# Layer norm, hedgehog linear attention and a SwiGLU layer in one kernel: casts of wo, output copies, norms and x stores put at other places in the queues

## The chip, the cores and the metric

The kernel runs on 1 core of one Trainium2 chip. The metric is the device time of one execution, in microseconds (us). The engines of a core are TensorE (PE, with its weight loads PEld), VectorE (DVE), ScalarE (ACT), GpSimd (POOL) and SyncE (SP), which here only issues DMAs. Each engine works through its own queue in order; semaphores make it wait for others.

## The reference

With S = 2048 rows, D = 576, 32 heads of 18 columns, and F = 4608, all in f32:

```python
xn = layernorm(x)                      # no gain, no bias
q, k, v = heads(xn @ wqkv)
pq, pk = q @ w_phi, k @ w_phi          # per head, 18x18
phi_q = concat(softmax(pq), softmax(-pq))
phi_k = concat(softmax(pk), softmax(-pk))
num = phi_q @ (phi_k.T @ v)
den = phi_q @ sum(phi_k) + 1e-6
s = (num / den) @ wo
g = silu((silu(x @ w_gate) * (x @ w_up)) @ w_down)   # this x is the normalised one
out = x + s * g
```

## The kernel before

Every f32 product is made of three products in the format fp32r. A number is split into a high part, which ScalarE casts, and a remainder, which VectorE or GpSimd subtracts (helpers `split`, `split_rows`): most steps below are such a cast and such a subtraction, ahead of matmuls.

The program has these stages, in order of time.

1. **Start, 0 to about 80 us.** x comes in four blocks of four row tiles, in the order 2, 3, 0, 1. For each block, `norm_stats` makes mean and variance on VectorE (bn_stats, L164, and bn_aggr, L165), a square root on ScalarE (L168) and two refinement steps. `norm_block` then normalises two tiles on VectorE (L181) and two on ScalarE (L178), copies the last 64 columns four times over on GpSimd (L184), transposes all on TensorE (L193), casts (ScalarE, L195) and subtracts (VectorE, L196) into the x operands `X`. A `fold` multiplies wk with w_phi (TensorE, L221), and `early_tile` computes tiles of the gate and up products, from weights that `early_weights` loads and splits. Block 2 is called the first block below, and block 3 the second.
2. **Keys and values, to about 228 us.** `k_tile` and `v_product` for 16 row tiles. `keep_x` stores three of the x operands (`a_dram`, 3 x 1280 KB) from SyncE's queue, for the last stage.
3. **Queries, about 228 to 480 us.** `q_tile` makes the feature map of 128 rows; its part `softmax_parts` takes a maximum (L278), a subtraction (L279), the same for the minimum, and two exponentials on ScalarE (L282). `numer` transposes and multiplies, `project` multiplies by wo and copies the output to `s_dram` through a ScalarE copy `so` (L619). `split_wo` casts wo in three pieces (WOH, WOL). Early tiles are laid between.
4. **Gate, up and down, about 480 us to the end.** `gate_up_weights` loads one unit's weights `ld` from SyncE's queue (L676), forms sums on GpSimd (L694 to L697), splits them (`w`) and stores them to `w_dram` (L687) for the second half of the rows; `gate_up` multiplies, with a ScalarE copy `snap` (L736) between products; the down products follow (`strassen`).

The order of each engine's queue is not the order of the text alone: a scheduler chooses among what is ready, and `tc.high_priority()` puts instructions ahead, while `tc.issue_after(x)` holds a group back until instruction x has been placed. Tiles of one name rotate among `bufs` buffers, so a new tile waits for the readers of an old one.

Of the kernel before, what the change touches and what calls it, by code (L numbers as in the profile page):

```python
# [46 lines left out]
def gated_hedgehog_kernel(ctx: ExitStack, tc, x, w_qk, w_v, w_phi, wo, w_gu, w_tail, w_down, ident_in, mask_in, out):  # L47
# [65 lines left out]
    def early_tile(f, i, parts, js=(0, 1), banks=None):  # L113
# [10 lines left out]
        return last  # L124

    with ExitStack() as att:
        const = att.enter_context(tc.tile_pool(name="const", bufs=1))
# [8 lines left out]
        with ExitStack() as wst:  # L136
# [4 lines left out]
            with ExitStack() as pst:  # L141
# [18 lines left out]
                def norm_stats(bs, xns):  # L160
# [11 lines left out]
                    nc.vector.scalar_tensor_tensor(r, q, 1.5, r, op0=ALU.add, op1=ALU.mult)  # L172
                    return nc.vector.scalar_tensor_tensor(q, mv[:, t, 0], -1.0, r, op0=ALU.mult, op1=ALU.mult)

                def norm_block(b, xns):
                    for n, (i, xn) in enumerate(zip(range(4 * b, 4 * b + 4), xns)):
                        if n % 2:
                            nc.scalar.activation(xn[:, 0:D], xn[:, 0:D], AF.Identity, bias=rt[:, i:i + 1],  # L178
                                                 scale=rs[:, i:i + 1])
                        else:  # L180
                            nc.vector.tensor_scalar(xn[:, 0:D], xn[:, 0:D], mv[:, i, 0:1], rs[:, i:i + 1],  # L181
                                                    op0=ALU.subtract, op1=ALU.mult)
                        for k in range(2):
                            nc.gpsimd.tensor_copy(xn[:, D + k * P:D + (k + 1) * P].rearrange("p (j n) -> p j n", j=4),  # L184
                                                  xn[:, 512 + 32 * k:544 + 32 * k].unsqueeze(1).to_broadcast([P, 4, 32]))
                    i, j = divmod(b, 2)
                    dst = XB[i][2 * j:2 * j + 2]
                    for c in range(3):
# [5 lines left out]
                        if c < 2:  # L194
                            nc.scalar.copy(dst[c][:, 0:2], ps)  # L195
                            nc.vector.tensor_sub(dst[c][:, 3:5], ps, dst[c][:, 0:2])  # L196
                            continue
# [75 lines left out]
            def softmax_parts(ps, e):  # L273
# [7 lines left out]
                for s in range(2):  # L281
                    nc.scalar.activation(e[:, s * D:(s + 1) * D], e[:, s * D:(s + 1) * D], AF.Exp,  # L282
                                         scale=1.0 if s == 0 else -1.0)
# [4 lines left out]
            kk_pool, read = kk, []  # L288

# [9 lines left out]
            def keep_x():  # L299
                for n, j in enumerate((0, 1, 3)):  # L300
                    nc.sync.dma_start(a_dram[n], XB[1][j].bitcast(F32))
# [17 lines left out]
            def sum_parts(k):  # L319
                r = raws[k]  # L320
                lo = los[k] = kk.tile([P, 4, 2, P], F32R, name="slo", bufs=1)
                for a in (2, 0):
# [5 lines left out]
                    nc.sync.dma_start(sum_dram[k // 4, :, j, k % 4, 0:3], hi.bitcast(F32))  # L328
                    nc.sync.dma_start(sum_dram[k // 4, :, j, k % 4, 3:5], lo[:, j].bitcast(F32))

# [97 lines left out]
            for p in range(8):  # L428
# [93 lines left out]
        with ExitStack() as qst:  # L522
# [75 lines left out]
            def project(b, oh, ol, last):  # L598
                for j in range(QS // P):
# [3 lines left out]
                    for i in range(2):  # L603
# [8 lines left out]
                        for g, (o, w) in enumerate(GROUPS):  # L612
                            for a, bw in ((oh, WOH), (oh, WOL), (ol, WOH)):
                                nc.tensor.matmul(ps[:, 0:HALF], a[0:w, g, jc], bw[0:w, g, n], start=k == 0,  # L614
                                                 stop=k == 3 * NG - 1)
                                k += 1
                        so = qk.tile([P, HALF], F32, name="so", bufs=2)
                        with tc.high_priority() if last else ExitStack():
                            nc.scalar.copy(so, ps[:, 0:HALF])  # L619
                        nc.scalar.dma_start(s_dram[r0:r0 + P, n], so)  # L620
# [408 lines left out]
    early_tile(EARLY - 1, 0, parts)  # L1029
    ready = [gate_up_weights(*todo.pop(0))]  # L1030
    est.close()
# [74 lines left out]
```

## Time and profile before

| | |
|---|---|
| time, median of 3 runs | 1636.75 us (1635.69 to 1640.77) |
| the profiled execution | 1638.38 us, its span 1636.6 us |
| TensorE busy | 1604.0 us (98%) |
| VectorE busy | 1168.5 us (71%) |
| ScalarE busy | 721.9 us (44%) |
| GpSimd busy | 653.3 us (40%) |
| DMA | 268.46 MB, mean 164 GB/s |

The span is the time from the first to the last instruction on the engines; 1.8 us of the execution lie around it. Busy times are sums over the whole span, and the stages differ: TensorE is without idle time for most of the program, and its idle time lies in a few places.

### The profile page before, as it was taken

To read this page: it belongs to the slowest core of one execution; us is meant where nothing else is said; L and a number is where in the kernel's file an instruction comes from. 1 tells how busy PE (TensorE), PEld (TensorE's weight loads), DVE (VectorE), ACT (ScalarE), POOL (GpSimd) and SP (SyncE) were. 2 spreads that over 40 slices of the span, in tenths; PEclk is the share of its full clock that TensorE was granted. 3 is DMA by queue.
4 is the path that set the end of the run, shared out by engine and by line. 5 is a ranking of instruction groups with operands and counts; after the bars stand their busy time and mean duration, and the time that the engine had idled before them with its cause. 6 is when DMAs were issued, how large, how long until landed. Compare 5 with 4: busy or idle time off the path is not lost.

```text
span 1636.6 us, 25198 instructions
## 1 busy us (share of the span) xinstructions
PE 1604.0 (98%) x9385; PEld 1429.7 (87%) x9385; DVE 1168.5 (71%) x1721; ACT 721.9 (44%) x1391; POOL 653.3 (40%) x699
## 2 busy tenths in 40 slices
PE   6999998999999999999999999999999999999998
PEld 5899997999978888888888888888888888888887
DVE  7677768899952678778777778825666766666578
ACT  5533345444432554544444544455433433333334
POOL 3485661333212455455545355313233324133132
PEclk9999999999999999999999999999999999999999
DMA  9622243334248545555554554684454655555444
GB/s 286 206 80 78 85 134 117 117 103 126 67 144 306 184 165 175 179 178 168 177 180 165 175 192 152 224 296 150 136 162 135 199 184 170 172 179 185 140 115 174
DMA packets 121741, 268.46 MB, mean 164 GB/s; under 512 B 12787, under 2 KB 53363, under 8 KB 119827
## 3 DMA queue, kind: packets, MB, share of 16 engines
q1 hardware_dynamic: 106652, 246.49, 45.9%
q0 software_dynamic: 3072, 11.02, 2.4%
q10 hardware_dynamic: 11894, 9.35, 1.8%
q8 instruction: 74, 1.21, 0.3%
q14 instruction: 49, 0.39, 0.1%
HBM read 167.19 MB, written 99.61 MB: 163 GB/s over the span
## 4 chain that ended last, share of the span: by engine, by line
PE 90%; DMA 4%; DVE 3%; POOL 1%; issue 1%; ACT 1%; SPq 0%; ACTq 0%; POOLq 0%; DVEq 0%
PE px L707 24%; PE pd L832 24%; PE pw L707 12%; PE py L707 6%; PE p L92 6%; PE pe L92 5%; PE p L614 4%; PE po L594 2%; PE kvp L294 2%; PE vx L382 1%; PE pt L588 1%; DMA xn<-in_A_x 1%; PE vw L382 1%; DMA s_dram<-so 1%; DMA sraw<-in_A_w_v 1%
## 5 line engine op out<-in xcount | busy, mean ns | idle before, releaser
L832 PEld LDWEIGHTS pd<-dw,hh 128*128 128x128 f32 x3048 | 432.4, 188 | 26.4 <-DVE dw L59 1.7
L832 PE MATMUL pd<-dw,hh 128*128 128x288 f32 x3048 | 448.5, 297 | 4.3 <-DVE dw L59 1.5
L707 PE MATMUL px<-X,w 128*128 128x512 f32 x1488 | 384.3, 393 | 0.0
L707 PEld LDWEIGHTS px<-X,w 128*128 128x128 f32 x1488 | 270.6, 188 | 51.8 <-ACT s L736 2.0
L707 PE MATMUL pw<-X,w 128*128 128x512 f32 x732 | 188.7, 393 | 0.0
L707 PEld LDWEIGHTS pw<-X,w 128*128 128x128 f32 x732 | 137.0, 188 | 30.5
L741 DVE TENSOR_TENSOR s<-pw,s 128x512 f32<-128x512 f32 x124 | 85.1, 688 | 100.0 <-ACT s L736 89.2
L957 DVE TENSOR_TENSOR acc<-pd,acc 128x576 f32<-128x576 f32 x128 | 96.2, 752 | 83.8 <-PE pd L832 83.6
L736 ACT COPY s<-px 128x512 f32<-128x512 f32 x124 | 72.6, 585 | 157.2 <-PE px L707 157.2
L92 PE MATMUL pe<-X,wh 128*128 128x512 f32 (+1 forms) x380 | 121.8, 401 | 5.8 <-ACT h L119 2.9
L59 DVE TENSOR_TENSOR hh<-ha,hh 128x512 fp32r<-128x512 f32 x140 | 111.5, 823 | 20.7 <-ACT hh L58 19.1
L58 ACT CAST hh<-ha 128x512 fp32r<-128x512 f32 x140 | 82.7, 619 | 92.4 <-PE pd L832 73.5
L929 POOL TENSOR_TENSOR hb<-hb 128x512 f32<-128x512 f32 x34 | 47.0, 1381 | 168.6 <-DVE hb L753 161.4
L59 DVE TENSOR_TENSOR w<-ld,w 128x512 fp32r<-128x512 f32 (+1 forms) x93 | 77.2, 832 | 35.7 <-ACT w L58 34.5
L707 PE MATMUL px<-X,wt 96*128 96x512 f32 x248 | 97.9, 395 | 0.0
L707 PE MATMUL py<-X,w 128*128 128x512 f32 x372 | 96.5, 394 | 0.0
L916 POOL TENSOR_TENSOR h<-ha,hb 128x512 f32<-128x512 f32 x34 | 44.3, 1302 | 126.8 <-DVE ha L757 88.6
L942 POOL TENSOR_TENSOR ha<-ha 128x512 f32<-128x512 f32 x34 | 52.6, 1564 | 103.5 <-DVE hh L59 103.5
L58 ACT CAST w<-ld 128x512 fp32r<-128x512 f32 (+1 forms) x93 | 51.0, 549 | 89.6 <-POOL ld L697 56.8
L92 PEld LDWEIGHTS pe<-X,wh 128*128 128x128 f32 (+1 forms) x380 | 70.0, 189 | 21.7 <-ACT h L119 3.4
L761 ACT COPY py<-px 128x512 f32<-128x512 f32 x62 | 35.5, 572 | 102.7 <-PE px L707 80.8
L707 PEld LDWEIGHTS py<-X,w 128*128 128x128 f32 x372 | 66.7, 188 | 11.2
(262 smaller groups left out, 3199.0 us busy)
## 6 DMA issues: line engine op xcount, KB each, us to landing
w_dram<-w SPq DMA_DIRECT2D x90, 512.0 KB, 2.9
w<-w_dram SPq DMA_DIRECT2D x90, 512.0 KB, 4.5
wt<-t_dram SPq DMA_DIRECT2D x61, 336.0 KB, 3.7
ld<-in_B_w_gu SPq DMA_DIRECT2D x31, 512.0 KB, 4.5
X<-sum_dram SPq DMA_DIRECT2D x8, 1280.0 KB, 11.1
rt<-in_B_w_down SPq DMA_DIRECT2D x33, 288.0 KB, 3.1
rb<-in_B_w_down SPq DMA_DIRECT2D x33, 288.0 KB, 4.7
w_dram<-w SPq DMA_DIRECT2D x30, 256.0 KB, 2.1
```

Source lines behind the costliest of these rows:

```text
L58: nc.scalar.copy(hi, src)
L59: nc.vector.tensor_sub(lo, src, hi)
L92: last = nc.tensor.matmul(ps, l, r, start=n == 0, stop=n == len(pairs) - 1)
L614: nc.tensor.matmul(ps[:, 0:HALF], a[0:w, g, jc], bw[0:w, g, n], start=k == 0, stop=k == 3 * NG - 1)
L707: nc.tensor.matmul(ps, l, r, start=first and n == 0, stop=last and n == len(mm) - 1, skip_group_check=True)
L736: nc.scalar.copy(t, ps)
L741: nc.vector.tensor_add(t, ps, t)
L832: nc.tensor.matmul(ps, l, r, start=first and n == 0 and m == 0, stop=n == len(hs) - 1 and m == 2, skip_group_check=True)
L916: sub(s, g["h"][0][0], g["h"][0][1])
L929: nc.gpsimd.tensor_add(a21, a21, g["h"][1][1])
L942: sub(a12, a12, g["h"][0][0])
L957: nc.vector.tensor_add(a2, pd[:, :, 0:HALF], a2)
```

## The change

Five things are edited.

- `norm_block` runs its norms (L178, L181, L184) with priority.
- The second block's `norm_stats` is held back until the first block's last remainder (L196) is placed, in place of the last step of the first block's statistics; then it runs with priority, and stands ahead of the first early tile's weights in the text.
- `split_wo` is held back until the last exponential placed so far, in place of the last subtraction; the third piece of wo is loaded into a buffer of the name `e` instead of `ez`.
- `keep_x` is held back until the preceding `sum_parts` has been placed.
- The last projection's last two output copies use a buffer of the name `e`, and the first unit's `gate_up_weights` is held back until the last output copy.

```diff
+    outs = []
...
-                    return nc.vector.scalar_tensor_tensor(q, mv[:, t, 0], -1.0, r, op0=ALU.mult, op1=ALU.mult)
+                    nc.vector.scalar_tensor_tensor(q, mv[:, t, 0], -1.0, r, op0=ALU.mult, op1=ALU.mult)
 
                 def norm_block(b, xns):
-                    for n, (i, xn) in enumerate(zip(range(4 * b, 4 * b + 4), xns)):
...
+                    with tc.high_priority():
+                        for n, (i, xn) in enumerate(zip(range(4 * b, 4 * b + 4), xns)):
...
-                            nc.vector.tensor_sub(dst[c][:, 3:5], ps, dst[c][:, 0:2])
+                            rest = nc.vector.tensor_sub(dst[c][:, 3:5], ps, dst[c][:, 0:2])
...
+                    return rest
...
-                chain = norm_stats([2], xns[0:4])
-                norm_block(2, xns[0:4])
+                norm_stats([2], xns[0:4])
+                rest = norm_block(2, xns[0:4])
+                with tc.issue_after(rest.ins), tc.high_priority():
+                    norm_stats([3], xns[4:8])
                 first_weights = [early_weights(0)]
-                with tc.issue_after(chain.ins):
-                    norm_stats([3], xns[4:8])
...
-                    nc.scalar.activation(e[:, s * D:(s + 1) * D], e[:, s * D:(s + 1) * D], AF.Exp,
-                                         scale=1.0 if s == 0 else -1.0)
+                    last = nc.scalar.activation(e[:, s * D:(s + 1) * D], e[:, s * D:(s + 1) * D], AF.Exp,
+                                                scale=1.0 if s == 0 else -1.0)
+                exps.append(last)
...
-                sum_parts(order[p - 1])
+                done = sum_parts(order[p - 1])
                 load_stack(order[p])
                 if p == 3:
-                    keep_x()
+                    with tc.issue_after(done.ins):
+                        keep_x()
...
-                   qk.tile([P, 2, D], F32, name="ez", bufs=1)]
+                   qk.tile([P, 2 * D], F32, name="e", bufs=4).rearrange("p (a n) -> p a n", a=2)]
...
-                with tc.issue_after(read[-1].ins):
+                with tc.issue_after(exps[-1].ins):
                     for n, wr in enumerate(wrs):
...
-                        so = qk.tile([P, HALF], F32, name="so", bufs=2)
+                        if last and i:
+                            so = qk.tile([P, 2 * D], F32, name="e", bufs=4)[:, 0:HALF]
+                        else:
+                            so = qk.tile([P, HALF], F32, name="so", bufs=2)
                         with tc.high_priority() if last else ExitStack():
-                            nc.scalar.copy(so, ps[:, 0:HALF])
+                            outs.append(nc.scalar.copy(so, ps[:, 0:HALF]))
...
-    ready = [gate_up_weights(*todo.pop(0))]
+    with tc.issue_after(outs[-1].ins):
+        ready = [gate_up_weights(*todo.pop(0))]
```

What it does to the queues is read from the order of each engine's instructions. In the rows of the changed kernel the line numbers are its own: from line 126 on they are 1 to 10 higher than those of before.

First the start. VectorE's row, before, at the end of the first block's statistics (`rt` is the bias of the norms on ScalarE, `X_64` and `X_65` are x operands):

```order
L172 SCALAR_TENSOR_TENSOR rs<-rt,rs 128x4
L173 SCALAR_TENSOR_TENSOR rt<-mv,rs 128x4
L181 TENSOR_SCALAR xn<-xn,mv,rs 128x576 x2
L164 BN_STATS stats<-xn 128x6 x2
L196 TENSOR_TENSOR X_64<-tp,X_64 128x1024
L196 TENSOR_TENSOR X_65<-tp,X_65 128x1024
L165 BN_AGGR mv<-stats 128x2
```

and now:

```order
L173 SCALAR_TENSOR_TENSOR rs<-rt,rs 128x4
L183 TENSOR_SCALAR xn<-xn,mv,rs 128x576 x2
L174 SCALAR_TENSOR_TENSOR rt<-mv,rs 128x4
L198 TENSOR_TENSOR X_64<-tp,X_64 128x1024
L198 TENSOR_TENSOR X_65<-tp,X_65 128x1024
L165 BN_STATS stats<-xn 128x6 x3
L166 BN_AGGR mv<-stats 128x2
```

The two norms L181 (now L183) stand ahead of the last step of the statistics L173 (now L174), and the two remainders L196 (now L198) ahead of the second block's first bn_stats.

ScalarE's row there, before, for the second block (its root is L168, its norms are those of `xn_135` and `xn_139`; `wh_346` is the weight of the second early tile, `wst` a piece of w_v):

```order
L168 ACTIVATE rs_104<-mv_103 128x4
L249 CAST KVWH_94<-wst_359 128x576
L249 CAST KVWH_94<-wst_361 128x576
L62 CAST wh_346<-raw_345 128x768
L62 CAST KVWH_94<-tp_274 128x6x126
L62 CAST KVWH_94<-tp_284 128x6x72
L119 ACT_TABLE_LOAD
L119 ACTIVATE h_608<-pe_592 128x512
L178 ACTIVATE xn_135<-xn_135,rt_105,rs_104 128x576
L178 ACTIVATE xn_139<-xn_139,rt_105,rs_104 128x576
```

and now, where the cast of `wh_346` is the row just ahead of these, and the two norms L180 end the piece and follow it:

```order
L119 ACT_TABLE_LOAD
L119 ACTIVATE h_608<-pe_592 128x512
L169 ACT_TABLE_LOAD
L169 ACTIVATE rs_104<-mv_103 128x4
L62 CAST KVWH_94<-tp_274 128x6x126
L62 CAST KVWH_94<-tp_284 128x6x72
L252 CAST KVWH_94<-wst_361 128x576
L252 CAST KVWH_94<-wst_363 128x576
L252 CAST KVWH_94<-wst_365 128x576
L252 CAST KVWH_94<-wst_367 128x576
L252 CAST KVWH_94<-wst_369 128x576
L180 ACTIVATE xn_135<-xn_135,rt_105,rs_104 128x576
```

The root, now L169, has moved behind the cast of `wh_346`, a SiLU and two table loads, and five casts of w_v stand ahead of the norms.

Second the first query tiles. VectorE's row before (`e_2461` is the first tile's result, `h_4768` the product of an early tile):

```order
L278 TENSOR_REDUCE m_2462<-p2_2432 128x32
L279 TENSOR_TENSOR e_2461<-p2_2432,m_2462 128x576
L278 TENSOR_REDUCE m_2462<-p2_2432 128x32
L279 TENSOR_TENSOR e_2461<-p2_2432,m_2462 128x576
L122 TENSOR_TENSOR h_4768<-pe_4753,h_4768 128x512
L63 TENSOR_TENSOR wl_4788<-raw_4786,wh_4787 128x512
```

and now:

```order
L281 TENSOR_REDUCE m_2462<-p2_2432 128x32
L122 TENSOR_TENSOR h_4768<-pe_4753,h_4768 128x512
L282 TENSOR_TENSOR e_2461<-p2_2432,m_2462 128x576
L281 TENSOR_REDUCE m_2462<-p2_2432 128x32
L282 TENSOR_TENSOR e_2461<-p2_2432,m_2462 128x576
L63 TENSOR_TENSOR wl_4788<-raw_4786,wh_4787 128x512
```

The product L122 has moved between the first maximum, L278 (now L281), and its subtraction, L279 (now L282).

Third the first units of the last stage. SyncE's row before (`ld_5468` holds the third unit's weights):

```order
L123 DMA h_dram_69<-h_5285 128x512
L676 DMA ld_5468<-in_B_w_gu 128x4x256
L123 DMA h_dram_69<-h_5319 128x512
L890 DMA rt_5560<-in_B_w_down 128x576
L890 DMA rb_5562<-in_B_w_down 128x576
L890 DMA rt_6118<-in_B_w_down 128x576
L890 DMA rb_6120<-in_B_w_down 128x576
L687 DMA w_dram_72<-w2_5383 128x1024
L687 DMA w_dram_72<-w2_5387 128x1024
L676 DMA ld_5566<-in_B_w_gu 128x4x256
```

and now:

```order
L696 DMA w_dram_72<-w2_5350 128x1024
L696 DMA w_dram_72<-w2_5354 128x1024
L696 DMA w_dram_72<-w1_5358 128x512
L696 DMA w_dram_72<-w2_5374 128x1024
L696 DMA w_dram_72<-w2_5383 128x1024
L696 DMA w_dram_72<-w2_5387 128x1024
L696 DMA w_dram_72<-w1_5391 128x512
L685 DMA ld_5468<-in_B_w_gu 128x4x256
L732 DMA ha_5463<-h_dram_69 128x512
L732 DMA hb_5464<-h_dram_69 128x512
```

The load of `ld_5468`, L676 (now L685), has moved behind all stores of the first two units' weights to `w_dram`.

More of the change, by code (lines that the diff above doesn't have):

```diff
@@ L172, in norm_stats @@
                     nc.vector.scalar_tensor_tensor(r, q, 1.5, r, op0=ALU.add, op1=ALU.mult)
-                    return nc.vector.scalar_tensor_tensor(q, mv[:, t, 0], -1.0, r, op0=ALU.mult, op1=ALU.mult)
+                    nc.vector.scalar_tensor_tensor(q, mv[:, t, 0], -1.0, r, op0=ALU.mult, op1=ALU.mult)
                 def norm_block(b, xns):
-                    for n, (i, xn) in enumerate(zip(range(4 * b, 4 * b + 4), xns)):
[L177 to L185, printed above, removed]
+                    with tc.high_priority():
+                        for n, (i, xn) in enumerate(zip(range(4 * b, 4 * b + 4), xns)):
+                            if n % 2:
+                                nc.scalar.activation(xn[:, 0:D], xn[:, 0:D], AF.Identity, bias=rt[:, i:i + 1],
+                                                     scale=rs[:, i:i + 1])
+                            else:
+                                nc.vector.tensor_scalar(xn[:, 0:D], xn[:, 0:D], mv[:, i, 0:1], rs[:, i:i + 1],
+                                                        op0=ALU.subtract, op1=ALU.mult)
+                            for k in range(2):
+                                nc.gpsimd.tensor_copy(xn[:, D + k * P:D + (k + 1) * P].rearrange("p (j n) -> p j n", j=4),
+                                                      xn[:, 512 + 32 * k:544 + 32 * k].unsqueeze(1).to_broadcast([P, 4, 32]))
                     i, j = divmod(b, 2)
@@ L286, in softmax_parts @@
                 return sm
-            kk_pool, read = kk, []
+            kk_pool, read, exps = kk, [], []
             def kv_step(n, phi, v):
@@ L328, in sum_parts @@
                     nc.sync.dma_start(sum_dram[k // 4, :, j, k % 4, 0:3], hi.bitcast(F32))
-                    nc.sync.dma_start(sum_dram[k // 4, :, j, k % 4, 3:5], lo[:, j].bitcast(F32))
+                    done = nc.sync.dma_start(sum_dram[k // 4, :, j, k % 4, 3:5], lo[:, j].bitcast(F32))
+                return done
             V1, V2 = slice(D + HALF, 2 * D), slice(D, D + HALF)
```

1 line of the change is left out of this document (added).

## The prediction

> **What bounds the kernel now.** The page comes first: the busy line of the engines.
>
> ```profile
> PE 1604.0 (98%) x9385; PEld 1429.7 (87%) x9385; DVE 1168.5 (71%) x1721; ACT 721.9 (44%) x1391; POOL 653.3 (40%) x699
> ```
>
> TensorE is busy for 1604.0 of 1636.6 us, so all that any reordering can win is the other 32.6 us. The second view, the waits of TensorE, says who ends them (columns: total us, times, longest).
>
> ```profile
> PE tp L193 <- DVE xn L181: 11.4, 2, 10.4
> PE pe L92 <- ACT h L119: 2.9, 4, 1.2
> PE pe L92 <- DVE h L122: 1.8, 2, 1.6
> PE tp L221 <- DVE X L196: 1.8, 1, 1.8
> PE pd L832 <- DVE dw L59: 1.5, 1, 1.5
> PE p L92 <- DVE e L279: 1.4, 1, 1.4
> PE p L614 <- ACT so L619: 1.2, 1, 1.2
> PE pd L832 <- DVE hh L59: 1.1, 1, 1.1
> ```
>
> 10.4 us of the first row is the wait for the first x rows, which the edit does not shorten. What it can reach is the rest of these rows, about 11.7 us. The third view, the windows, says where the rest of the program stands (span start:end, length, PE busy, then PEld, DVE, ACT, POOL, granted clock, DMA share, GB/s).
>
> ```profile
> 260.00:280.00 20.00, 18.08 (x106) 15.59 (x107) 19.62 (x33) 9.84 (x14) 0.00 (x0) 1.00 0.21 67
> 560.00:1636.00 1076.00, 1068.85 (x5876) 942.35 (x5874) 758.10 (x1081) 475.36 (x931) 415.13 (x369) 1.00 0.54 174
> ```
>
> From 560 us on TensorE idles 7.15 us in 1076, nearly all of it at the very end, and the orders of all engines are the same there before and after. So whatever TensorE has gained or lost by 560 us comes out at the end one for one. In 260 to 280 us VectorE is busy for 19.62 of 20: there it is VectorE's order that decides.
>
> The edit reorders three stretches, costed in turn: the start (0 to 80 us), the first query tiles (228 to 275) and the last projection with the first gate-up units (464 to 560).
>
> **The start: what goes.** The timelines of VectorE and of TensorE (start, length, instruction, in brackets the idle time before it and what ended it):
>
> ```profile
> 15.64 0.82 DVE L164 BATCH_NORM_STATS2 stats<-xn 128x6 f32<-128x288 f32 x2 [4.76 <-DMA xn<-in_A_x]
> 16.38 2.34 DVE L196 TENSOR_TENSOR X<-tp,X 128x1024 fp32r<-128x1024 f32 x2
> ...
> 17.64 5.91 PE L221 MATMUL tp<-PHI,wst 126*128 126x126 f32 x36 [1.83 <-DVE X L196]
> 33.47 3.46 PE L193 MATMUL tp<-ident,xn 128*128 128x128 f32 x24 [0.92 <-DVE xn L181]
> 53.58 0.50 PE L92 MATMUL pe<-X,wh 128*128 128x512 f32 x1 [0.82 <-ACT h L119]
> ```
>
> Two bn_stats of the second block, waiting for their DMA until 15.64, stand on VectorE ahead of the two remainders L196, and TensorE's fold waits 1.83 us for the first remainder. In the new order both remainders stand ahead of all bn_stats of that block. Their input is a ScalarE cast:
>
> ```profile
> 9.93 1.63 ACT L178 ACTIVATE xn<-xn,rt,rs 128x576 f32<-128x576 f32 x2 [1.16 <-DVE rt L173]
> 13.07 1.01 ACT L195 CAST X<-tp 128x1024 fp32r<-128x1024 f32 x1 [1.51 <-PE tp L193]
> ```
>
> The norm on ScalarE waits for rt (L173), which now stands behind the two L181, so the chain to this cast is about 1.1 us later: the cast ends at 15.15 instead of 14.08, the first remainder at 15.15 + 1.17 = 16.3, and the fold starts there instead of at 17.64: 1.3 us won. The granted clock adds to it (windows of 2 us, TensorE alone):
>
> ```profile
> 16.00:18.00 2.00, 0.36 (x3) 1.00 1.01 384
> 18.00:20.00 2.00, 2.00 (x16) 0.72 0.69 261
> 20.00:22.00 2.00, 2.00 (x11) 0.50 0.62 152
> 22.00:24.00 2.00, 2.00 (x16) 0.93 1.14 322
> ```
>
> After the gap of 1.83 us the clock falls: the loss is 2 x (0.28 + 0.50 + 0.07) = 1.7 us. With the gap cut to about half a us I take the clock as kept. TensorE is then 1.3 + 1.7 = 3.0 us ahead when the fold's first three groups are through.
>
> The Trainium skill (TensorE: Matmul & The Clock Gate, Part 1: The HAM clock gate) has the array at half rate after an idle window of about 3.4 us. The trace only partly agrees, since here 1.83 us were enough. By that rule read strictly the drop was none of this gap's doing, and the 1.7 us would not be won.
>
> **The start: what it costs.** Those 3.0 us go into a wait for the second block, whose norms are now late. ScalarE and SyncE before:
>
> ```profile
> 28.28 0.83 ACT L62 CAST wh<-raw 128x768 fp32r<-128x768 f32 x1 [1.71 <-DMA raw<-in_B_w_gu]
> ...
> 30.24 1.28 ACT L119 ACT_TABLE_LOAD   x1
> 31.54 0.60 ACT L119 ACTIVATE h<-pe 128x512 f32<-128x512 f32 x1
> 32.03 1.61 ACT L178 ACTIVATE xn<-xn,rt,rs 128x576 f32<-128x576 f32 x2
> ...
> 22.99 0.84 SPq L106 DMA_DIRECT2D raw<-in_B_w_gu  x2
> 31.76 0.36 SPq L301 DMA_DIRECT2D a_dram<-X  x1
> ```
>
> In the new order ScalarE's square root for that block (L168) stands behind the cast of the second early tile's weights wh_346, which waits for a DMA, behind a table load, a SiLU and another table load. The DMA took 28.28 - 22.99 = 5.3 us; its buffer is free again some 1.5 us sooner than before (the 1.3 of the fold, carried to the remainder that frees it), so it lands at about 26.8. Then 0.83 + 1.28 + 0.60 + 1.28 lead to 30.8 for the root. VectorE's rest of the chain, with a fold remainder and the product L122 now in between, takes an estimated 2.9 us (two rows of 0.7 and some nine short ones), and the first L181 ends near 34.2. Before it ended just ahead of the transposes at 33.47. The two norms on ScalarE (L178) follow seven casts: 30.8 + 7 x 0.62 = 35.1, and end at 36.8 instead of 33.64. Twelve of the 24 transposes (3.46 / 2 = 1.7 us) need them, so the last ends near 38.5, where before it ended at 33.47 + 3.46 = 36.9: 1.6 us behind. About 0.2 of it is caught up in the short waits that follow there, leaving 1.4.
>
> Against that, the three x stores (a_dram, the first at 31.76) leave SyncE's queue in this stretch for about 150 us, where nothing waits for them. They hold 3 x 1.28 MB, and the loads of the next x blocks and weights go out ahead; I take the later 0.82 us at 53.58 as won. The start as a whole: 1.4 - 0.8 = **+0.6 us**. Bounds: -4 if the second block's chain is hidden after all, +4 if it is later by two more us and the clock falls behind it.
>
> **The query tiles.** VectorE and ScalarE before:
>
> ```profile
> 234.51 0.76 DVE L279 TENSOR_TENSOR e<-p,m 128x576 f32<-128x576 f32 x1
> ...
> 240.32 0.69 DVE L122 TENSOR_TENSOR h<-pe,h 128x512 f32<-128x512 f32 x1 [3.59 <-ACT e L282]
> ...
> 253.47 0.69 DVE L63 TENSOR_TENSOR wl<-raw,wh 128x512 fp32r<-128x512 f32 x1 [4.94 <-ACT wh L62]
> ...
> 269.46 0.75 DVE L279 TENSOR_TENSOR e<-p,m 128x576 f32<-128x576 f32 x1
> 252.62 0.82 ACT L62 CAST wh<-raw 128x768 fp32r<-128x768 f32 x1
> ```
>
> The `wo` casts go behind the second tile's exponentials, which takes two DMA waits of ScalarE out of the way of those exponentials. But VectorE's product L122, which cannot start before TensorE's tile ends at 240.3, now stands between the first reduction and the first L279 of the first query tile. The tile's bank is free when both L279 are done: 240.32 + 0.69 + three rows of 0.7 = 243.1. TensorE's second query tile, which before followed the early tile at once, now waits for it: a new wait of 2.8 us. Next on VectorE the subtraction L63 behind the 252.62 cast stands ahead of the second tile's L279, so it again idles until about 253.4. VectorE's idle time is then (240.32 - 234.5) + 3.4 = 9.2 us where it was 3.59 + 4.94 = 8.5; the work is the same, but 3.5 us of wo remainders now lie between these and the third tile. Followed through row by row, the third tile's last L279 ends near 271.9 instead of at 270.2, and TensorE's wait that ends there (the 1.4 us row above) ends 1.6 us later. What it waits for earlier in the stretch is swallowed by this one. **+1.6 us**, bounds 0 (if the exponentials' head start takes all of it) and +2.8 (the new wait in full).
>
> The stretch after it, in the view of the windows:
>
> ```profile
> 275.00:464.00 189.00, 188.99 (x1297) 173.82 (x1297) 170.84 (x269) 84.72 (x153) 54.48 (x112) 1.00 0.31 95
> ```
>
> TensorE has no idle time there, and VectorE is idle for 18.2 of 189 us; I take 0, up to +1 since that slack is thin.
>
> **The last projection and the first units.**
>
> ```profile
> 476.97 0.62 ACT L58 CAST w<-ld 128x512 fp32r<-128x512 f32 x1 [3.22 <-DMA ld<-in_B_w_gu]
> ...
> 481.18 0.40 ACT L619 COPY so<-p 128x288 f32<-128x288 f32 x1 [3.29 <-DMA s_dram<-so]
> ...
> 529.52 0.58 ACT L736 COPY s<-px 128x512 f32<-128x512 f32 x1
> ...
> 507.42 0.55 SPq L676 DMA_DIRECT2D ld<-in_B_w_gu  x1
> ...
> 522.23 0.55 SPq L676 DMA_DIRECT2D ld<-in_B_w_gu  x1
> ...
> ld<-in_B_w_gu SPq DMA_DIRECT2D x31, 512.0 KB, 4.5
> ```
>
> The first cast of gate-up weights waits for its DMA until 476.97 with the output copy behind it, and the third copy waits until 481.18 for a store to give its buffer back. With the copies ahead and two more buffers, the 1.2 us row (L614) and the 0.9 us of SiLU waits after it go, less some 0.2 for the new order: -1.9. The two waits of the rows L832 (1.5 + 1.1) lie at 540 us, where VectorE splits weights for the first down products; with two of those casts earlier I let 2.5 of them go. The price lies on SyncE: the third unit's weights, issued at 507.42, now stand behind all stores of the first two units, the last of which needs a remainder made at about 521. They go out near 522.5, as the next unit's do before, land 4.5 us later at 527, need four GpSimd subtractions (about 3.3 us, to 530.3), and then two casts stand on ScalarE ahead of the snapshot that ran at 529.52: 530.3 + 0.4 + 0.6 + 0.58 = 531.9 instead of 530.1. I take **2.0 us** for this new wait, bounds 0 and 4. Together -1.9 - 2.5 + 2.0 = **-2.4 us**, bounds -4.5 and +1.
>
> **The sum.** +0.6 + 1.6 - 2.4 = -0.2 us. The profiled execution took 1638.38 us, its span of 1636.6 and 1.8 around it, 1.6 above the median of the three runs. Against its own time the sum gives 1638.2; on the median of 1636.75 the forecast is **1636.5 us**. A measurement of this kernel can tell about 0.3%, or 4.9 us, from no change.
>
> **The rivals.**
> 1. *Faster: the second block is not late.* If the weights of the second early tile land three us sooner, since the stores no longer share the DMA engines, the root runs near 28, the norms are ready before TensorE, and the 3.0 us won at the fold stay, with the 0.92 at 33.47 and the 0.8 at 53.58: -4.5 in place of +0.6, and -5.3 with the others: 1631.4; with the whole of the 4.7 us in the last stretch kept and the snapshot's wait half hidden, 1629.9. For it: the x stores are 3.84 MB in the busiest DMA stretch. Against: before, the loads in question were issued ahead of the first store. Chance 0.24.
> 2. *Slower: ScalarE's square root of the second block waits longer.* Place: the root behind the wh_346 cast. Every us that its DMA lands after 26.8 costs one, and TensorE, idle from about 30 (its work before 32.5, less the 3.0) to 34, then pays a clock drop as it does after 1.83 us at 16: 1.7. It decides from a landing about 3.5 us later, at 30.3: -0.2 + 3.5 + 1.7 = +5.0, 1641.7. For it: the windows at 16 to 24 us above show a DMA share of 0.62 to 1.14, the engines nearly full. Against: before, the same load landed at 28.28. Chance 0.17. The skill's 3.4 us rule on the clock, cited above, would have the drop there, since this gap is longer than its window.
> 3. *A smaller shift: the third unit's weights decide.* The wait on the snapshot is 4 us and the two waits at 540 us stay: -1.9 + 4 for the last stretch, +4.3 in all, 1641.0, still within 0.3%. Chance 0.12.
> 4. *The edit does not do what it says:* the waits change names, and each stretch ends where it ended because the DMA sets it: 1636.7. Chance 0.10.
>
> **How the numbers follow.** My forecast, the sum within its bounds, has 0.37. With rivals 3 and 4 the chance of within 0.3% is 0.59; faster 0.24, slower 0.17. The range of 8 in 10 goes from rival 1's far end to just past rival 2: 1629.9 to 1642.0.
>
> **What would show it.** Right: the fold starts near 16.3 and the clock stays at 1.00 through 24 us; a wait of some 4 us ahead of the transposes at 34; a wait of 2 to 3 us for VectorE's L279 at 243; no wait at L614; the third unit's load issued after 520 and a wait on the snapshot near 530. Wrong: transposes at 31 or earlier, no wait at 243, or the third unit's load going out ahead of the stores. A TensorE that is level with the order before at 560 us but ends elsewhere would mean that the unchanged part reacts to something not seen here.

## The result, and the profile after

The changed kernel takes 1649.7 us (median of 6 runs, 1648.12 to 1650.9) where the kernel before took 1638.09 beside it: a ratio of 1.0071, with a 95% interval of 1.0058 to 1.0084, or 11.6 us slower (9.5 to 13.8). The forecast of 1636.5 and the range up to 1642.0 were wrong. Below, a ratio is given in us as well, as its distance from 1 times 1638 us.

The profiled execution took 1648.54 us with a span of 1646.4, which is 9.8 us more than before. The busy line of its page, and the first rows of TensorE's waits:

```profile
PE 1609.6 (98%) x9385; PEld 1435.0 (87%) x9385; DVE 1172.1 (71%) x1721; ACT 724.8 (44%) x1393; POOL 654.2 (40%) x699
...
PE tp L195 <- DVE xn L183: 13.3, 2, 10.5
PE px L716 <- ACT s L745: 4.9, 2, 3.8
PE tp L224 <- ACT wh L62: 3.1, 1, 3.1
PE p L92 <- DVE e L282: 2.9, 2, 1.7
```

TensorE is busy for 5.6 us longer with the same 9385 matmuls, and idle for 4.2 us longer. So more than half of the loss is not a wait: the same work ran slower. The granted clock shows where; here are the windows of the three stretches in which it was lower (0 to 80, 228 to 280 and 530 to 570 us), whose clock column was 0.98, 1.00 and 1.00 before.

```profile
0.00:80.00 80.00, 61.81 (x349) 53.75 (x350) 53.05 (x120) 47.77 (x62) 28.48 (x53) 0.94 0.62 187
...
228.00:280.00 52.00, 48.41 (x263) 41.89 (x262) 37.21 (x55) 25.43 (x35) 22.86 (x31) 0.97 0.53 168
...
530.00:570.00 40.00, 34.55 (x161) 28.89 (x160) 25.62 (x32) 18.93 (x38) 22.59 (x22) 0.96 0.65 223
```

Two instructions with a fixed place in the program say how far the kernel had got: the first matmuls of L505 (now L511), ahead of the query tiles, and the first gate-up product L707 (now L716). The lines stand in the order before, after, before, after; the first kind is from the view of one source line, the second from TensorE's timeline.

```profile
L505 PE MATMUL p<-ident,zc x16: 275/275/319, 227.5 to 229.2; 126*128 126x126 f32 x16
L511 PE MATMUL p<-ident,zc x16: 275/275/319, 233.7 to 235.4; 126*128 126x126 f32 x16
512.84 1.55 PE L707 MATMUL px<-X,w 128*128 128x512 f32 x6
517.09 1.53 PE L716 MATMUL px<-X,w 128*128 128x512 f32 x6
```

The start lost 6.2 us (forecast 0.6). The query tiles and the projection gave back 6.2 - 4.25 = 1.9 together (forecast 1.6 - 1.9 = -0.3). From the first gate-up product to the end 9.8 - 4.25 = 5.5 were lost (forecast -0.5), 4.6 of them by 570 us, where the same matmuls run 8.85 us later than before.

These shares come from one trace of each kernel and are rough. In the traces of four kernels below whose start is not edited (d_wo, d_out, wo_out, u_start) the first mark lies between 225.8 and 230.9 us, and in three others that have the edits of the start (d_start, u_wo, u_hold) between 230.7 and 233.0.

**The start, after.** TensorE's timeline (the fold, its fourth group, the second block's transposes), then ScalarE's (the cast of wh_346, the root, the last of the five w_v casts, the norms):

```profile
16.62 4.67 PE L224 MATMUL tp<-PHI,wst 126*128 126x126 f32 x36
27.88 4.41 PE L224 MATMUL tp<-PHI,wst 126*128 126x126 f32 x24 [3.07 <-ACT wh L62]
38.12 0.66 PE L195 MATMUL tp<-ident,xn 128*128 128x128 f32 x2 [2.74 <-DVE xn L183]
...
26.42 0.83 ACT L62 CAST wh<-raw 128x768 fp32r<-128x768 f32 x1 [2.98 <-DMA raw<-in_B_w_gu]
30.48 0.20 ACT L169 ACTIVATE rs<-mv 128x4 f32<-128x4 f32 x1
35.35 0.67 ACT L252 CAST KVWH<-wst 128x576 fp32r<-128x576 f32 x1 [0.21 <-DMA wst<-in_A_w_v]
38.66 1.63 ACT L180 ACTIVATE xn<-xn,rt,rs 128x576 f32<-128x576 f32 x2 [2.64 <-DVE rt L174]
```

The fold starts at 16.62 with no gap, as forecast (16.3), and the root comes at 30.48, as forecast (30.8). But the transposes start at 38.12 and not at 34.2. VectorE's timeline (the first remainder of the fold, the statistics of the next block, the product, the norms) and the windows of the clock:

```profile
27.35 0.42 DVE L64 TENSOR_TENSOR KVWH<-tp,KVWH 32x252 fp32r<-32x252 f32 x1
...
31.41 1.18 DVE L165 BATCH_NORM_STATS2 stats<-xn 128x6 f32<-128x288 f32 x3
...
35.42 0.69 DVE L122 TENSOR_TENSOR h<-pe,h 128x512 f32<-128x512 f32 x1 [1.12 <-PE pe L92]
...
36.80 1.66 DVE L183 TENSOR_SCALAR xn<-xn,mv,rs 128x576 f32<-128x576 f32 x2
...
28.00:30.00 2.00, 2.00 (x10) 0.50 0.99 368
30.00:32.00 2.00, 2.00 (x15) 0.72 0.37 94
...
38.00:40.00 2.00, 1.08 (x4) 0.50 0.78 229
40.00:42.00 2.00, 2.00 (x12) 0.50 0.78 230
42.00:44.00 2.00, 2.00 (x11) 0.50 0.72 221
44.00:46.00 2.00, 2.00 (x10) 0.81 0.47 121
```

This is a ring. TensorE waits 3.07 us for a fold remainder of VectorE, and then runs at half clock. (The row names the cast of wh_346, which ended at 27.25. But the group starts 0.11 us behind the end of the remainder L64, and in five other kernels below, d_start, r_after, e_mul, e_casts and e_all, 0.09 to 0.10 us behind it; in r_after and e_mul it starts before that cast has ended.) VectorE's product L122 waits for a tile that TensorE makes after this, until 35.42, with the norms behind it. TensorE waits 2.74 us for the norms, and again runs at half clock for some 6 us.

The two falls cost 2 x (0.50 + 0.28) = 1.6 us and, since TensorE was busy for only 1.08 of the 2 us from 38 on, 1.08 x 0.50 + 2 x (0.50 + 0.50 + 0.19) = 2.9 us: together 4.5 where the one before cost 1.7. TensorE's idle time grew by 2.6 us up to 80 us, from 15.55 to 18.19, and by 0.7 from there to 228. With the 2.8 us by which the clock costs more, that makes 6.1 of the 6.2 us.

The casts of w_v, which stand ahead of ScalarE's norms, did not hold these up: the last of them ends at 36.02, and the norms wait until 38.66 for VectorE's last step rt (L174), which stands behind VectorE's norms.

**The first units, after.** SyncE, GpSimd, ScalarE and TensorE:

```profile
532.63 6.23 SPq L696 DMA_DIRECT2D w_dram<-w  x4
538.92 0.76 SPq L899 DMA_DIRECT2D rb<-in_B_w_down  x1
...
545.13 1.02 POOL L926 TENSOR_TENSOR td<-rb,rt 128x288 f32<-128x288 f32 x1
...
552.11 0.43 ACT L58 CAST dw<-td 128x288 fp32r<-128x288 f32 x1 [4.98 <-POOL td L933]
...
554.82 0.58 ACT L745 COPY s<-px 128x512 f32<-128x512 f32 x1
...
536.09 1.65 PE L716 MATMUL px<-X,w 128*128 128x512 f32 x6 [1.10 <-ACT s L745]
...
555.46 1.85 PE L716 MATMUL px<-X,w 128*128 128x512 f32 x6 [3.77 <-ACT s L745]
```

The rows of w_down (`rb`) go out at 538.92, behind four stores of the third unit's weights; before, they went out at 514.59, ahead of these. GpSimd's sums of them begin at 545.13, where before they began at 518.81. Three sums of the fourth unit's weights stand ahead of the last of them, which ends at 552. A ScalarE cast waits for it, and the snapshot behind that cast holds TensorE for 3.77 us. The third unit's own wait, which the forecast put at 2.0, is the 1.10.

With a third wait of 0.58 us these make 5.45 us in place of 2.6, and the clock falls behind the last one (0.69, 0.50 and 0.96 in the windows of 2 us from 556 on): 2 x (0.31 + 0.50 + 0.04) = 1.7 us. Together this is the 4.6 us that were lost here. GpSimd itself does not wait for `rb` in this trace, since it is busy with other sums from 542.18 on; its order has changed along with SyncE's, and no run below changes one without the other.

### The profile page after: what moved, and what is told of

It reads as the page before. It is cut to its first block, busy times and chain, and to the rows that moved or that the text cites. A ratio compares the mean times of both kernels' runs of the same rounds, so it can differ in the third digit from the quotient of the medians.

```text
span 1646.4 us, 25195 instructions
## 1 busy us (share of the span) xinstructions
PE 1609.6 (98%) x9385; PEld 1435.0 (87%) x9385; DVE 1172.1 (71%) x1721; ACT 724.8 (44%) x1393; POOL 654.2 (40%) x699
## 4 chain that ended last, share of the span: by engine, by line
PE 65%; DVE 1%; ACT 0%; issue 0%; ACTq 0%; DVEq 0%
PE pd L841 24%; PE px L716 23%; PE pw L716 11%; PE py L716 6%; DVE acc L813 0%; DVE acc L814 0%; ACT w L58 0%; ACT hh L58 0%; DVE w L59 0%; DVE hh L59 0%; DVE hb L762 0%; DVE s L750 0%; DVE X L966 0%; DVE ha L766 0%; ACT acc L812 0%
## 5 line engine op out<-in xcount | busy, mean ns | idle before, releaser
L716 PE MATMUL px<-X,w 128*128 128x512 f32 x1488 | 384.7, 393 | 4.9 <-ACT s L745 4.9
L716 PEld LDWEIGHTS px<-X,w 128*128 128x128 f32 x1488 | 270.5, 188 | 57.2 <-ACT s L745 7.5
L716 PE MATMUL pw<-X,w 128*128 128x512 f32 x732 | 188.6, 393 | 0.0
L716 PEld LDWEIGHTS pw<-X,w 128*128 128x128 f32 x732 | 137.0, 189 | 30.4
L716 PE MATMUL px<-X,wt 96*128 96x512 f32 x248 | 98.2, 396 | 0.0
L716 PE MATMUL py<-X,w 128*128 128x512 f32 x372 | 96.7, 394 | 0.6 <-ACT py L770 0.6
L716 PEld LDWEIGHTS py<-X,w 128*128 128x128 f32 x372 | 66.7, 188 | 12.1 <-ACT py L770 0.9
```

Source lines behind the costliest of these rows:

```text
L716: nc.tensor.matmul(ps, l, r, start=first and n == 0, stop=last and n == len(mm) - 1, skip_group_check=True)
```

## The experiments

**Each part alone**, on the kernel before.

The two edits of the start (d_start):

```diff
-                    for n, (i, xn) in enumerate(zip(range(4 * b, 4 * b + 4), xns)):
+                    with tc.high_priority():
+                        for n, (i, xn) in enumerate(zip(range(4 * b, 4 * b + 4), xns)):
...
+                with tc.issue_after(rest.ins), tc.high_priority():
+                    norm_stats([3], xns[4:8])
                 first_weights = [early_weights(0)]
-                with tc.issue_after(chain.ins):
-                    norm_stats([3], xns[4:8])
```

> The kernel before with the edits of the start alone: the norms with priority, and the second block's statistics held behind the first block's last remainder, with priority. Theory A, that the loss of the whole change is made mostly at the start: the trace of the changed kernel stands 5.5 us behind at the first kvp product, so this kernel is slower by 5 to 6 us, with the clock at 0.50 from about 28 and again from about 38 us. Theory B, that the start is about neutral and the loss is made in the first gate-up units: within 1.5 us of the kernel before.

Measured: 1.0044 (1.0032 to 1.0057), +7.2 us, with the clock at 0.91 over the first 80 us. Theory A holds: the edits of the start alone make most of the loss.

The wo edits (d_wo):

```diff
-                with tc.issue_after(read[-1].ins):
+                with tc.issue_after(exps[-1].ins):
...
-                   qk.tile([P, 2, D], F32, name="ez", bufs=1)]
+                   qk.tile([P, 2 * D], F32, name="e", bufs=4).rearrange("p (a n) -> p a n", a=2)]
```

> The kernel before with the wo edits alone: the wo casts held behind the second tile's exponentials, and the third piece of wo in a buffer named e. In the order of SyncE this alone moves the first down-projection rows and the fourth unit's weights behind the stores of the first units. Theory A, that those loads decide the first units, and not the held gate-up weights: a wait of 2 to 4 us for the snapshot near 550 us, and in all 0 to 4 us slower, since the wo edit itself may give back 1 to 2 us in the query tiles. Theory B, that the held gate-up weights are the cause: no such wait, 1 to 2 us faster.

Measured: 1.0009 (1.0000 to 1.0018), +1.5 us, at the edge of what can be told. TensorE waits 3.05 us for the snapshot at 549, as theory A has it: an edit of the query tiles alone brings a wait into the first units. Since the two waits of 1.1 and 1.5 us at 540 fall to 0.2, the net is small.

The output edits (d_out):

```diff
-                        so = qk.tile([P, HALF], F32, name="so", bufs=2)
+                        if last and i:
+                            so = qk.tile([P, 2 * D], F32, name="e", bufs=4)[:, 0:HALF]
+                        else:
+                            so = qk.tile([P, HALF], F32, name="so", bufs=2)
...
-    ready = [gate_up_weights(*todo.pop(0))]
+    with tc.issue_after(outs[-1].ins):
+        ready = [gate_up_weights(*todo.pop(0))]
```

> The kernel before with the output edits alone: two output copies in buffers named e, and the first unit's gate-up weights held behind the last output copy. SyncE's order of the later units is nearly that of the kernel before. Theory A (the loads moved by the wo edit are the cause of the loss there): no wait for the snapshot, the 2 us of waits around the last projection gone, 1 to 3 us faster. Theory B (the held weights are the cause): 3 to 5 us slower, with a wait for the snapshot between 530 and 560 us.

Measured: 0.9992 (0.9983 to 1.0001), -1.3 us: at the edge of what can be told, and not 3 to 5 us slower. The held weights alone are not the cause. One wait of 1.00 us for the snapshot stands at 524, which theory A did not have.

The later x stores (d_keep):

```diff
-                    keep_x()
+                    with tc.issue_after(done.ins):
+                        keep_x()
```

> The kernel before with the x stores alone put later. My prediction took 0.8 us for it at 53.58 us: 0.5 to 1 us faster. The rival, that the stores matter to nothing: within 0.5 us.

Measured: 0.9996 (0.9987 to 1.0005). That is -0.7 us (-2.1 to +0.8). The wait of 0.82 us at 53.58 is gone from its trace, but a gain of 0.8 us can be told neither from this nor from none, so the run does not decide.

The four alone add up to 7.2 + 1.5 - 1.3 - 0.7 = 6.7 us, where the whole change costs 11.6. So some parts may cost more together; the runs that follow test this.

**One part taken back**, from the changed kernel.

The edits of the start (u_start), the wo edits (u_wo), and the hold on the first unit's weights (u_hold), each by its diff above read the other way, the last as

```diff
-    with tc.issue_after(outs[-1].ins):
-        ready = [gate_up_weights(*todo.pop(0))]
+    ready = [gate_up_weights(*todo.pop(0))]
```

> The changed kernel with the edits of the start taken back, the other edits kept. Alone, the start cost 7.3 us, the wo edit 1.5, the output edit -1.3, the x stores 0; together 7.5, where the whole change costs 11.6. Theory I (the missing 4 us come from the wo edit and the held weights together, in the first units): 1642 us, with the wait for the snapshot near 550 us still at 3 to 4 us. Theory II (they come from the late start shifting all that follows): 1638 to 1639 us, and that wait is gone.

Measured: 1.0019 (1.0010 to 1.0027), +3.1 us, with waits for the snapshot of 1.32 and 3.79 us. Theory I: the missing part is there without the late start.

> The changed kernel with the wo edits taken back. Theory I: 1644.4 us (the start's 7.3 less the output edit's 1.3), no wait of over 1.5 us for the snapshot between 530 and 570 us. Theory II: 1648 us.

Measured: 1.0027 (1.0018 to 1.0036), +4.4 us, one wait for the snapshot, of 1.01 us. The same verdict, though 1.5 us less than the parts alone make (7.2 - 1.3 = 5.9).

> The changed kernel with the first unit's gate-up weights no longer held behind the last output copy; the output copies keep their e buffers. Theory I: 1645 to 1647 us, the wait for the snapshot shorter than 3.8 us. Theory II: 1649 to 1651 us, the wait unchanged.

Measured: 1.0048 (1.0035 to 1.0060), +7.9 us, the wait 3.04 us. Theory I again; but most of this one wait is there without the hold. What goes with the hold is the wait of 1.10 us.

The wo and the output edits together, and nothing else, on the kernel before (wo_out):

> The kernel before with the wo edits and the output edits together, and nothing else. If parts added up: 1.5 - 1.3 = 0.2 us slower. Theory I (the two together put the third and fourth units' loads behind all stores of the first units): 3 to 5 us slower, with waits for the snapshot of over 1 and over 3 us between 525 and 560 us. Theory II (the missing part needs the late start): within 1.5 us of the kernel before.

Measured: 1.0034 (1.0021 to 1.0046), +5.6 us, where the two alone make 0.2. In SyncE's order of this kernel, as in that of the changed one, all eight stores of the first two units stand ahead of the third unit's load, and the four of the third unit ahead of `rb`. Its TensorE timeline:

```profile
530.18 1.65 PE L712 MATMUL px<-X,w 128*128 128x512 f32 x6 [1.32 <-ACT s L741]
539.63 1.33 PE L837 MATMUL pd<-dw,hh 128*128 128x288 f32 x8 [0.58 <-DVE dw L59]
549.54 2.93 PE L712 MATMUL px<-X,w 128*128 128x512 f32 x6 [3.76 <-ACT s L741]
```

Waits of 5.7 us in place of 2.6, and 2.93 us for matmuls that take 1.54 at full clock: theory I holds, the waits come without the late start. The kernel u_start has the same edits, and the later x stores besides, and shows nearly the same waits; it measured +3.1 us (1.6 to 4.4) against 3.4 to 7.5 here. So the pair costs some 3 to 6 us. That the loads' place in SyncE's order does it is read from the traces; no run moves the loads alone.

**The two edits of the start apart**, on the kernel before: the norms' priority (d_prio), and the held statistics (d_stats), each by its lines of the first diff.

> The kernel before with the priority of the norms alone. In its order the second block's square root stays where it was, ahead of the cast of wh_346. Theory A (the loss of the start comes from the held statistics, which put the root and VectorE's last steps late): within 1.5 us of the kernel before, no wait of over 2 us ahead of the second block's transposes. Theory C (the norms' priority is the cause, since the bias step behind the two VectorE norms delays ScalarE's norms): 3 to 7 us slower.

Measured: 0.9998 (0.9989 to 1.0007), no change that can be told: theory C falls.

> The kernel before with the held statistics alone (held behind the first block's last remainder, with priority, ahead of the first early tile's weights). In its order the root stands behind the cast of wh_346 and two table loads. Theory A: 5 to 7 us slower, with waits of 2 to 4 us around the second block's transposes and the clock at 0.50 there. Theory C: within 2 us.

Measured: 1.0008 (0.9999 to 1.0017), +1.3 us. Theory A falls too: neither edit costs 5 us alone, and the 7.2 appear only with both. VectorE's and TensorE's timelines of d_stats:

```profile
31.07 0.69 DVE L122 TENSOR_TENSOR h<-pe,h 128x512 f32<-128x512 f32 x1
...
33.66 1.07 DVE L181 TENSOR_SCALAR xn<-xn,mv,rs 128x576 f32<-128x576 f32 x2
...
34.39 3.11 PE L193 MATMUL tp<-ident,xn 128*128 128x128 f32 x18 [3.35 <-DVE xn L181]
```

Here the product L122 stands behind VectorE's last step for the scale (L172) and finds its tile ready, though it does stand ahead of the norms. TensorE is not late with that tile: the fold's fourth group starts at 24.67 without a wait.

**What closes the ring**, in four runs on the changed kernel.

The second early tile's casts behind the root (r_after; `roots` collects the square roots):

```diff
-                first_weights.append(early_weights(1))
+                first_weights.append(early_weights(1, roots[1]))
```

> The changed kernel with one more hold: the second early tile's casts (wh_346 among them) behind the second block's square root, so that the root no longer waits on ScalarE for that weight's DMA. Theory A (the root's place is the cause of the loss at the start): the root at 26 to 28 us instead of 30.5, the second block's transposes 3 to 4 us sooner, and 1645 to 1647 us. Theory B (VectorE's rows and the wait of the fold's fourth group set the start): the transposes within 1 us of 38.1, and 1649 to 1650 us.

Measured: 1.0056 (1.0044 to 1.0068), +9.2 us, 2.4 less than the change. The root comes at 27.53, 3 us sooner, but the transposes only at 36.70 instead of 38.12: between the theories. VectorE still has a product and remainders ahead of the norms. In u_hold and u_wo, which have the edits of the start but not this hold, the transposes start at 36.74 and 35.21, so the 1.4 us may not come from the hold.

The product L122 of the first early tile behind VectorE's second norm (e_mul):

```diff
-            with tc.high_priority():
-                nc.vector.tensor_mul(h, pu, h)
+            with tc.issue_after(behind.ins) if behind and j == 0 else ExitStack():
+                with tc.high_priority():
+                    nc.vector.tensor_mul(h, pu, h)
```

> The changed kernel with the first early tile's product L122 held behind the second block's two norms on VectorE, so that these no longer wait, through it, for TensorE. Theory P (the two engines wait for each other there: the product waits for TensorE's tile until 35.4, the norms for the product, the transposes for the norms): the transposes start about 1.5 us sooner than at 38.1 and the kernel is 1.5 to 3 us faster than the changed one (8.5 to 10 us over the kernel before). Theory Q (the root alone matters): no change, 11 to 12 us over the kernel before.

Measured: 1.0048 (1.0035 to 1.0061), +7.9 us, 3.8 less than the change; the transposes start at 35.46, but only two of them: the other 22 start at 38.40, where they started at 39.58.

That, and the w_v casts behind ScalarE's norms (e_casts):

```diff
-                    nc.scalar.copy(vh, src)
+                    with tc.issue_after(an3.ins):
+                        nc.scalar.copy(vh, src)
```

> As e_mul, and the casts of w_v on ScalarE held behind its two norms of the second block. Theory P: ScalarE's norms run right behind the root's last step, in the place where VectorE's run; 1 to 2 us better than e_mul. Theory Q: as e_mul.

Measured: 1.0038 (1.0024 to 1.0051), +6.2 us, 5.4 less than the change; the transposes start at 33.62 and the other 22 at 35.12, earlier than in any of the four kernels with the edits of the start alone or beside others (37.76 in u_wo to 39.64 in d_start). But the reason is not theory P's. ScalarE's norms wait for VectorE's last step rt here too (4.05 us), as they did with the casts ahead of them (2.64). What has moved along with the casts is GpSimd's subtraction of w_v (L254), beside which VectorE was slow; the last section comes back to it.

All three (e_all):

> As e_casts, and the second early tile's casts held behind the root. Theory P: all that the start lost is given back and the gap at the fold is gone, so the start is level with the kernel before or up to 2 us ahead, and the kernel is 3 to 5 us over the kernel before, which is what the wo and output edits cost together. Theory Q: the same, with e_mul and e_casts at the changed kernel's time and this one alone better.

Measured: 1.0040 (1.0027 to 1.0053), +6.6 us, no better than e_casts. The gap at the fold is not gone: the fourth group waits 2.00 us, the clock stands at 0.50 from 28 to 34 us, and the transposes start at 35.60. Less what the other edits cost together (5.6 us in wo_out, 3.1 in u_start), 1 to 3.5 us are left to the start. So theory Q falls, since e_casts too is clear of the changed kernel. Theory P holds in that the product's hold and the casts' hold together give back most of the start's loss; that the ring is all of it is not shown. The intervals of these four overlap in part, so the steps between neighbours are rough; from the change to e_casts and e_all they do not overlap.

**A version that might beat both**: priority of the norms and the output edits (prio_out).

> A version that may beat both: the kernel before with the norms' priority and the output edits (e buffers and held gate-up weights), without the wo edit, the held statistics and the later x stores. If parts add up: 1 to 2 us faster than the kernel before; if theory C of the norms holds, slower by 2 us or more.

Measured: 0.9993 (0.9984 to 1.0002), -1.1 us. This is no gain that can be told from none.

## Why the prediction was wrong

- **That the end shifts one for one with 560 us** held, but for 0.9 us: the shift is 8.85 us at 570, and 9.7 behind one new wait of 0.63 us at 830.
- **What the edit can reach:** the rows without the 10.4 us add up to 12.7 us and not 11.7. The 1.0 left out is what remains of the first row, mainly the wait of 0.92 us at 33.47, and it is the wait that grew, to 2.74. That all that a reordering can win lies in TensorE's idle time was not right either: its busy time grew by 5.6 us.
- **The start, what goes:** right. The gap of 1.83 us went, the fold came at 16.62, and the clock stayed at 1.00 through 26 us. TensorE was 2.3 us ahead when the first three groups were through (21.05 in place of 23.31), where I took 3.0.
- **The start, what it costs:** this step failed, by 5.6 us. The root's time was right to 0.3 us. The mis-sized term is "VectorE's rest of the chain", an estimated 2.9 us: from the root's end to the start of the norms it took 36.80 - 30.68 = 6.1 us. Five bn_stats of the next block, 2.0 us, stand there that I did not count, and the product L122 waited 1.12 us for its tile, where I had counted its own 0.69 us as though the tile were ready. These two make the difference. The tile comes from TensorE, which I had taken to be ahead; it stood 3.07 us at the fold's fourth group, a wait that I did not see. I followed each engine with the others' times as they were before, and so missed the ring. With the product's hold 3.8 us go (e_mul, whose interval overlaps that of the change), with that and the casts' hold 5.4.
- **The norms on ScalarE:** I put them behind seven casts, to end at 36.8. They ended at 40.3, behind VectorE's last step and not behind the casts.
- **The clock:** I priced one fall as won and none as lost in the sum; rival 2 had the fall behind the new gap, with 1.7 us. At the start it came twice, for 4.5 us, and then once more in the query tiles (1.5) and in the first units (1.7). By the rule of the Trainium skill that I cited (TensorE: Matmul & The Clock Gate, Part 1: The HAM clock gate), a gap of 3.07 us could have been short enough. The trace fell after it, and after 2.74.
- **The wait of rival 2** was the right one, its trigger was not: the weights landed at 26.4, as in the sum, and not at 30.3.
- **The query tiles:** the predicted new wait for L279 came, at 249.48, which is 243.3 on the old time, with 1.65 us in place of 2.8. What I did not price is the clock behind it, 0.50 and 0.76 from 250 to 254 us: 2 x (0.50 + 0.24) = 1.5 us. The wo edits alone cost 1.5 us in all (0.0 to 2.9).
- **The last projection:** the output waits went, as forecast, and alone the output edits measured -1.3 us (-2.8 to +0.2).
- **The first units:** this step failed as well, by some 5 us (4.6 lost by 570 us, forecast -0.5). SyncE's order was read rightly, and the two waits at 540 fell from 2.6 to 0.6 us, nearly as forecast. But only the third unit's load was priced (2.0; measured 1.1). The rows of w_down were moved past the same stores, and by the trace they cost 3.77 us one unit later, through GpSimd and ScalarE, in front of a snapshot. Rival 3 named the place and the bound of 4 us, but not that the clock falls behind it.
- **The x stores:** 0.8 us taken. The wait went; whether the time did is open (-2.1 to +0.8 us).

## What to carry to other kernels

When an order changes, follow the chain across engines with the new times, not the old: an instruction that waits for another engine costs what stands behind it on its own, and two such waits can close a ring. Here two pairs of edits that were nearly harmless alone cost some 3 to 7 us together, so sum edits only after reading the joint order. List every row between two steps, those of other blocks too, and every transfer that a queue moves past another, not just the first one.

## What the runs showed of the hardware

**The clock falls after gaps of different lengths, and not always.** Three pieces of TensorE's timeline and two windows: before, u_wo, and d_wo.

```profile
542.23 1.33 PE L832 MATMUL pd<-dw,hh 128*128 128x288 f32 x8 [1.50 <-DVE dw L59]
```

```profile
544.31 2.29 PE L840 MATMUL pd<-dw,hh 128*128 128x288 f32 x8 [1.50 <-DVE dw L59]
```

```profile
549.08 1.66 PE L708 MATMUL px<-X,w 128*128 128x512 f32 x6 [3.05 <-ACT s L737]
...
546.00:548.00 2.00, 0.03 (x1) 1.00 0.86 273
548.00:550.00 2.00, 0.92 (x4) 1.00 0.48 196
```

After the same gap of 1.50 us the same eight matmuls took 1.33 us in one kernel and 2.29 in another, and after 3.05 us of idling the clock stayed at 1.00 in a third. The Trainium skill, in the section cited above, calls the window that the gate watches free-running. That fits, since then the phase decides; no run here shows the phase itself.

**VectorE slows down beside GpSimd.** VectorE's remainder of a weight (L64, 32x256) takes 0.42 us in most places; in the changed kernel two of them ran while GpSimd worked (the two lines of POOL):

```profile
20.84 1.40 DVE L64 TENSOR_TENSOR wh<-raw,wh 32x256 fp32r<-32x256 f32 x1
...
23.69 1.58 DVE L64 TENSOR_TENSOR wh<-raw,wh 32x256 fp32r<-32x256 f32 x1
...
18.99 2.96 POOL L205 TENSOR_TENSOR X<-xr,X 32x512 fp32r<-32x512 f32 x2 [5.62 <-ACT xr L203]
23.58 1.42 POOL L254 TENSOR_TENSOR KVWL<-wst,KVWH 128x576 fp32r<-128x576 f32 x1 [1.62 <-ACT KVWH L252]
```

They took 1.0 and 1.2 us longer, ahead of the remainder that the fold's fourth group waited for. The Trainium skill (GPSIMD Engine Reference, 1. Specifications) has the two engines contend when VectorE reads two inputs from SBUF, as this one does, and the trace agrees. So does e_casts: there GpSimd stands idle from 21.15 us on, and the second remainder takes 0.42 us. That it made part of the 3.07 us is read from the trace; it was not tried by itself.
